# A direct second layer for the fourth token tile of a retention block with a two-layer network, and its groups prepared further ahead

## The chip, the cores and the metric

The kernel runs on one core of a Trainium2 chip. The core has a matrix engine (PE; its weight loads are listed apart as PEld), a vector engine (DVE), an activation engine (ACT), a general engine (POOL), and a queue engine (SP) that issues most of the DMA transfers. Each engine works through its own list of instructions in order; semaphores make one wait for another. The metric is the device time of one execution in microseconds (us). Unless said otherwise, times in the text are counted from the first instruction of the profiled execution.

## The reference

Eight batches of 576 tokens, eight heads of 64. For each head: scores q k^T / 8, multiplied by a decay gamma^(i-j) for j <= i and 0 else, times v. The heads side by side give x with 4608 rows and 512 columns, which goes through two layers:

```python
def _attn_ref(q, k, v):
    scores = scale * np.matmul(q, k.transpose(0, 1, 3, 2))
    ret = scores * Dmat[None, :, :, :]        # gamma[h] ** (i - j), lower triangle
    return np.matmul(ret, v)

def _moe_ref(x, w_in, w_out):                 # w_in 512x2048, w_out 2048x512
    h = x @ w_in
    g = h * np.cos(h)
    return g @ w_out
```

Inputs and output are float32; the kernel multiplies in bfloat16 and sums in float32.

## The kernel before

**Groups.** The 4608 tokens are 36 groups of 128. `load` (L117) issues the DMAs of a group's q, k and v on SP, 256 KB each; group 22 and three others lie across two batches and are loaded in halves. `prep` scales q and k by powers of gamma (L140) and casts v to bfloat16 (L156), on POOL, in the later groups with the cast on ACT. `transposes` (L167) brings the scaled q and k into the layout of the score matmuls; from group 6 on this is one DMA transpose per group, issued on SP, which waits for POOL's two scalings. Five buffers hold raw q, k, v; eight hold prepared groups.

**Attention.** `scores` (L195, then the masked copy on DVE, L207), `state` and `states` (L231, L266: the running sum of k^T v, added up on DVE, L285 and L287) and `attn_out` (L333 `own`, L319 `carried`, then a copy to `xT` on ACT, L350). `scores2(g)` makes the scores of two groups in the banks a and b. `unit7(g, ...)` makes the states of g+1 and g+2, the output of groups g and g+1, and, where `more` is true, the scores of g+2 and g+3.

**Token tiles.** Ten tiles, of 512, 256, 256 and seven times 512 rows; they are numbered from 0, so tile 3 has rows 1024 to 1535 and its groups are 8 to 11. For each tile comes the first layer, `mm1` (eight blocks: PE L365, cosine on ACT L373, product to `gT` on DVE L374), and then the second. Tiles 0 to 2 have a direct second layer (`mm2`, L382): for each of the row blocks of 128, sixteen matmuls of 512 columns are summed in one bank, copied by ACT and stored, and `feed(s)` follows. Attention for the next tile is put between these matmuls by a list `todo` of positions. Tiles from `S7` = 3 on make the product g @ w_out from seven products of half size (`mm2_seven`, L517: 112 matmuls of 256 columns). These need sums of quarters of w_out (`w_sums`, DVE L418, two of them written over w_out itself) and of gT (`g_sum`, L445, on POOL, some on DVE). `sums_after(n, i)` says behind which block of the first layer these are issued; in the tiles after the first two of the seven-product kind the second halves follow in `late_sums`, at the second product. The products come in the order 3, 4, 5, 2, 1, 7, 6, and a dictionary `at` says ahead of which of them attention is put.

**What sets the order.** Nothing is rescheduled: every engine keeps the order in which the program was written (`manual_schedule`). So SP's queue has loads, transposes and stores in the order in which `feed` and the stores issue them, and POOL has preparations and sums in the order of the calls. `feed(s)`, called at each store of row block s, prepares groups up to a number that depends on s, issues their transposes, and then loads further groups. On SP each transfer also waits until the one eight places ahead has landed. PSUM has tags a, b, m (two banks each) and n, st (one each); a block of the first layer holds its tag until DVE's product is done.

Of the kernel before, what the change touches and what calls it, by code (L numbers as in the profile page):

```python
# [17 lines left out]
def kernel(  # L18
# [16 lines left out]
    nc = tc.nc  # L35
    P = 128
# [17 lines left out]
    assert sum(widths) == NTOK  # L54
    starts = [sum(widths[:n]) for n in range(len(widths))]
    N_PE_T = 6
    S7 = 3
    LD = 5

    consts = ctx.enter_context(tc.tile_pool(name="consts", bufs=1))  # L60
# [70 lines left out]
    def prep(g, early=False, kv_first=False):  # L131

        c = g % PER
        fk, fv = (tiles.pop(("f" + n, g)) for n in "kv")
        qks = nat.tile([P, 2, H, D], BF16, tag="qks", name="qks")
        vb = nat.tile([P, H, D], BF16, tag="vb", name="vb")
        qkT = trp.tile([P, 2 * HG, P], BF16, tag="qkT", name="qkT")

        def scaled(eng, m, f, by):
            eng.tensor_tensor(  # L140
                out=qks[:, m].rearrange("p (b a) d -> p a b d", a=2),
                in0=f.rearrange("p (a b) d -> p a b d", a=2),
                in1=by[:, c, :].rearrange("p (a b) -> p a b", a=2).unsqueeze(3).to_broadcast(
                    [P, 2, HG, D]
                ),
                op=ALU.mult,
            )

        if not early and not kv_first:
            scaled(nc.gpsimd, 0, tiles.pop(("fq", g)), gq)  # L150
        scaled(nc.vector if g == 3 else nc.gpsimd, 1, fk, gk)
        if early:
            tiles["fv", g] = fv
        else:
            copy_v = nc.scalar.copy if g > starts[S7] // P + 17 else nc.gpsimd.tensor_copy
            copy_v(vb, fv)  # L156
            if c == MIX and g > PER:
                copy_v(v_odd[HP:, g // PER % 2], fv[HP:])
        if kv_first:
            scaled(nc.gpsimd, 0, tiles.pop(("fq", g)), gq)  # L160
        qT = qT4[:, :, g * P : (g + 1) * P] if early else qkT[:, :HG, :]
        tiles["a", g] = (qks, vb, qkT, qT)
# [213 lines left out]
    def mm2(n, tsi, et):  # L376
        gT = tiles["g", n]
        if et == 0:
            bank = {0: "nmnm", 1: "nm", 2: "mn"}[n][tsi]
            tiles["o", tsi] = psum.tile([P, DM], F32, tag=bank, name="o")  # L380
        ps = tiles["o", tsi]
        nc.tensor.matmul(  # L382
            ps,
            lhsT=gT[:, et, tsi * P : (tsi + 1) * P],
            rhs=w_out_sb[:, et, :],
            start=(et == 0),
            stop=(et == ET - 1),
        )
        if et == ET - 1:
            s = starts[n] // P + tsi  # L390
            ot = op.tile([P, DM], F32, tag="oabcd"[1 + s % 4], name="ot")
            nc.scalar.copy(ot, ps)  # L392
            nc.sync.dma_start(out[s * P : (s + 1) * P, :], ot)
            feed(s)
# [30 lines left out]
    def g_sum(n, x, e0, e1):  # L425

        gT = tiles["g", n]
        a, b, op_ = {
            5: ((0, 0), (0, 1), ALU.add),
            2: ((1, 0), (1, 1), ALU.add),  # L430
            1: ((0, 0), (1, 1), ALU.add),
            7: ((0, 1), (1, 1), ALU.subtract),
            6: ((1, 0), (0, 0), ALU.subtract),
        }[x]
        if ("gs", n, x) not in tiles:
            tiles["gs", n, x] = sump.tile([P, E2, 256], BF16, tag=f"gs{x}", name=f"gs{x}")
        on_dve = x == 5 or (n, x) == (S7, 2) or (n, x, e0) in (
            (S7, 1, 4), (last, 1, 0), (last, 2, 4)
        )
        step = e1 - e0 if on_dve else 2  # L440
        for e in range(e0, e1, step):
            i0, i1 = (
                gT[:, k * E2 + e : k * E2 + e + step, r * 256 : (r + 1) * 256] for r, k in (a, b)
            )
            i = (nc.vector if on_dve else nc.gpsimd).tensor_tensor(  # L445
                out=tiles["gs", n, x][:, e : e + step], in0=i0, in1=i1, op=op_
            )
            if on_dve:
                tiles["gate"] = i
            elif "gate" in tiles:  # L450
                tc.add_manual_dep(
                    i.ins,
                    tiles.pop("gate").ins.name,
                    mybir.DependencyInfo(mybir.DependencyClass.Sync, mybir.DependencyReason.DATA),
                    reason="port free",
                )

    def sums_after(n, i):

        if n == S7:  # L460
            if i < 4:
                w_sums(3 + i % 2, i // 2 * 4, i // 2 * 4 + 4)
            elif i < 6:
                g_sum(n, 5, i % 4 * 4, i % 4 * 4 + 4)
                if i == 5:
                    g_sum(n, 6, 0, 4)
            elif i == 7:
                g_sum(n, 2, 0, E2)
                g_sum(n, 1, 4, E2)
                g_sum(n, 1, 0, 4)  # L470
                for e in (0, 4):
                    g_sum(n, 7, e, e + 4)
                prep_next(kv_first=True)
                g_sum(n, 6, 4, E2)
        elif n == S7 + 1 and i in (3, 7):
            for x in (5, 2, 1):
                g_sum(n, x, i - 3, i + 1)
            for x in (7, 6) if i == 7 else ():
                for e in (0, 4):
                    g_sum(n, x, e, e + 4)  # L480
        elif i == 3:
            for x in (5, 2, 1, 7, 6) if n < last else (5, 1, 2, 7, 6):
                g_sum(n, x, 0, 4)
        elif i == 7 and n == last:
            late_sums(n)
# [113 lines left out]
    def feed(s):  # L599

        nonlocal loaded, prepared, transposed
        before = loaded
        n, r = divmod(s - starts[S7] // P, 4)
        if n >= 0:
            while prepared < min(NG, starts[S7] // P + 10 + 4 * n + ((0, 1, 2, 4) if n else (-1, 0, 1, 4))[r]):
                prep_next()
            while transposed < prepared:
                transposes(transposed)
                transposed += 1
            ahead = starts[S7] // P + 14 if n == 0 and r < 3 else prepared + LD  # L610
            while loaded < min(NG, prepared + LD, ahead):
                load(loaded)
                loaded += 1
            return
        while True:
            while prepared < min(loaded, 2 * s + 7, s + 11, starts[S7] // P + 8):
                prep(prepared)
                prepared += 1
                if transposed < N_PE_T:
                    transposed += 1  # L620

            if N_PE_T <= transposed < min(prepared, s + 11) and (
                transposed <= loaded - 2 or loaded == NG or (s > 3 and loaded == before)
            ):
                transposes(transposed)
                transposed += 1
            elif loaded < min(NG, 2 * s + 8, s + 13):
                load(loaded)
                loaded += 1
            else:  # L630
                break
# [148 lines left out]
    for n, w in enumerate(widths):  # L780

        if n in (0, 3):
            halves = [(h, et) for et in range(0, ET, 4) for h in range(2)]
            if n == 3:
                halves.sort()
            blocks = [(et, half * 256, 256) for half, et in halves]
        elif n == 1:
            blocks = [(et, half * P, P) for half in range(2) for et in (0, 8)]
        else:
            m = 1024 // w  # L790
            blocks = [(et, 0, w) for et in range(0, ET, m)]
            if n > S7:
                blocks = [(e + k * E2, 0, w) for e in range(0, E2, m) for k in range(2)]
        banks = {0: "abmabmab", 1: "bmba", 2: "bmab", 3: "mamabmab"}.get(n, "abmabmab")
        for i, (et, c0, cw) in enumerate(blocks):
# [25 lines left out]
        elif n == 1:  # L821
            todo = pair(6, "ab", 16, 27)
        elif n == 2:
            todo = [(11, lambda: scores2(g)), (25, lambda: unit(g, "m", soon=True))]
            late += [lambda: unit(g + 2, "b", False)]
        else:
            at = {}
            if n + 1 < len(widths):
                at = {
                    4: lambda then, off: unit7(g, "st", True, lambda: late_sums(n), off),  # L830
                    1: lambda then, off: unit7(g + 2, "n", True, then),
                }
                if n in (3, 4):
                    at = {
                        5: lambda then, off: (then(), scores2(g)),
                        1: lambda then, off: unit7(g, "n", True, then),
                        6: lambda then, off: unit7(g + 2, "b", n > 3, then),
                    }
            mm2_seven(n, at)
            continue  # L840
        todo.sort(key=lambda u: u[0])
# [42 lines left out]
```

## Time and profile before

| | us |
|---|---|
| three runs | 299.29, 300.03, 300.26 |
| median | 300.03 |
| profiled execution, first to last instruction (its own time is given as this span) | 298.2 |
| busy in it: PE / DVE / ACT / POOL | 287.1 / 207.9 / 135.9 / 209.4 |
| first layer of tile 3 | 84.20 to 99.55 |
| second layer of tile 3 | 99.55 to 116.78 |
| tile 4 | 116.78 to 149.83 |
| tile 5 | 149.83 to 179.84 |
| tile 6 | 180.00 to 209.35 |

Busy time of PE counts modelled ends of matmuls that overlap, so the spacing of a dense row of matmuls (its time divided by their number) says what one costs, not the mean duration. In the timeline a line is start, duration, engine, line, operation, output <- inputs, shapes, count, and in brackets the idle time ahead with what ended it. SPq rows are issues; when a transfer lands is told apart from that, as "DMA to landing".

### The profile page before, as it was taken

What the parts mean: (1) busy time and instruction counts of PE and PEld (TensorE: products, weight loads), DVE (VectorE), ACT (ScalarE), POOL (GpSimd) and SP (SyncE); (2) the same over time, 40 slices, a digit from 0 to 9 for tenths busy, and PEclk for the clock granted to TensorE, in tenths of its full rate; (3) what the DMA queues carried; (4) which work ended last, traced back from release to release, by engine and by line L of the source; (5) the groups of instructions that cost most, each with busy time, mean ns of one, the idle gap of its engine ahead of it and who ended that gap; (6) DMA issues with size and microseconds to landing.
All of it is one profiled execution on the core that took longest, in us unless ns stands there. A gap on an engine that the chain in (4) does not pass through costs nothing.

```text
span 298.2 us, 7384 instructions
## 1 busy us (share of the span) xinstructions
PE 287.1 (96%) x3113; PEld 195.3 (65%) x3113; DVE 207.9 (70%) x245; ACT 135.9 (46%) x167; POOL 209.4 (70%) x214
## 2 busy tenths in 40 slices
PE   8899999999999999979999999999999999999995
PEld 3478646848578786448744875488448845874584
DVE  5677637564579994788848874887489757935872
ACT  2656433514255432642346554546464446425620
POOL 2750066436445599997999999599959946980693
PEclk9999999999999999999999999999999999999999
DMA  7999999999999999999999997998690260031013
GB/s 203 212 209 206 209 214 213 200 243 208 208 174 222 211 239 213 217 279 176 198 224 229 209 200 183 212 208 201 122 194 2 73 143 0 2 106 36 0 44 99
DMA packets 154304, 50.28 MB, mean 169 GB/s; under 512 B 140832, under 2 KB 153248, under 8 KB 154272
## 3 DMA queue, kind: packets, MB, share of 16 engines
q1 hardware_dynamic: 149504, 45.10, 77.2%
q0 software_dynamic: 4224, 4.19, 8.5%
q8 instruction: 24, 0.39, 0.6%
q10 hardware_dynamic: 544, 0.52, 0.5%
q14 instruction: 8, 0.07, 0.1%
HBM read 36.70 MB, written 9.44 MB: 155 GB/s over the span
## 4 chain that ended last, share of the span: by engine, by line
PE 43%; POOL 25%; SPq 13%; DMA 8%; DVE 5%; issue 3%; ACT 1%; POOLq 0%; DVEq 0%
PE h L365 22%; POOL gs L445 17%; PE o L517 11%; SPq L117 8%; POOL qks L140 6%; PE o L382 5%; SPq L167 4%; DVE gT L374 3%; DMA fk<-in_k_dram 2%; DMA w_in_sb<-in_moe_w_in_dram 2%; DMA qkT<-qks 2%; POOL vb L156 2%; DVE gs L445 2%; DMA fv<-in_v_dram 1%; ACT cosh L373 1%
## 5 line engine op out<-in xcount | busy, mean ns | idle before, releaser
L445 POOL TENSOR_TENSOR gs<-gT 128x512 bf16<-128x512 bf16 x102 | 116.3, 1180 | 29.4 <-DVE gs L445 29.4
L365 PE MATMUL h<-xT,w_in_sb 128*128 128x512 bf16 (+2 forms) x832 | 127.6, 313 | 2.6 <-DVE gT L374 1.8
L374 DVE TENSOR_TENSOR gT<-h,cosh 128x1024 bf16<-128x1024 f32 x72 | 87.8, 1223 | 43.7 <-ACT cosh L373 40.7
L373 ACT ACTIVATE cosh<-h,half_pi 128x1024 f32<-128x1024 f32 x72 | 80.2, 1114 | 72.2 <-PE h L365 69.8
L365 PEld LDWEIGHTS <-w_in_sb 128*128 128x128 bf16 x832 | 75.9, 98 | 51.6 <-issue 3.0
L140 POOL TENSOR_TENSOR qks<-fq,gq 128x512 bf16<-128x512 f32 x32 | 34.0, 1062 | 40.9 <-DMA fq<-in_q_dram 40.9
L517 PEld LDWEIGHTS <-gs 128*128 128x128 bf16 x576 | 53.6, 98 | 10.1 <-POOL gs L445 2.9
L140 POOL TENSOR_TENSOR qks<-fk,gk 128x512 bf16<-128x512 f32 x35 | 37.3, 1066 | 8.0 <-DMA fk<-in_k_dram 7.4
L207 DVE TENSOR_TENSOR ret<-sc,tri 128x1024 bf16<-128x1024 f32 x32 | 38.1, 1217 | 2.8 <-PE sc L195 2.7
L517 PE MATMUL o<-ws,gs 128*128 128x256 bf16 (+1 forms) x352 | 39.1, 268 | 0.7 <-POOL gs L445 0.5
L382 PE MATMUL o<-w_out_sb,gT 128*128 128x512 bf16 x128 | 30.1, 380 | 0.0
L517 PE MATMUL o<-w_out_sb,gT 128*128 128x256 bf16 x224 | 26.6, 273 | 0.1
L517 PE MATMUL o<-w_out_sb,gs 128*128 128x256 bf16 x224 | 26.1, 273 | 0.5 <-POOL gs L445 0.4
L537 DVE TENSOR_TENSOR ot<-o,ot 128x512 f32<-128x512 f32 (+2 forms) x25 | 14.9, 603 | 14.7 <-PE o L517 14.5
L517 PEld LDWEIGHTS <-gT 128*128 128x128 bf16 x224 | 21.4, 98 | 4.7 <-DVE gT L374 0.7
L350 ACT CAST xT<-ov 128x1024 bf16<-128x1024 f32 (+1 forms) x18 | 16.5, 917 | 16.1 <-PE ov L319 13.9
L445 DVE TENSOR_TENSOR gs<-gT 128x1024 bf16<-128x1024 bf16 (+1 forms) x18 | 20.4, 1148 | 0.3
L382 PEld LDWEIGHTS <-gT 128*128 128x128 bf16 x128 | 11.8, 98 | 12.5
L156 POOL CAST vb<-fv 128x512 bf16<-128x512 f32 x22 | 14.3, 651 | 4.4 <-DMA fv<-in_v_dram 4.2
L564 ACT COPY ot<-o 128x512 f32<-128x512 f32 x7 | 4.1, 586 | 20.5 <-PE o L517 20.5
L392 ACT COPY ot<-o 128x512 f32<-128x512 f32 x8 | 4.7, 588 | 17.4 <-PE o L382 17.4
L537 DVE TENSOR_TENSOR ot<-ot,o 128x512 f32<-128x512 f32 x14 | 9.6, 684 | 4.0 <-ACT ot L569 2.4
(70 smaller groups left out, 175.8 us busy)
## 6 DMA issues: line engine op xcount, KB each, us to landing
out_dram<-ot SPq DMA_DIRECT2D x35, 256.0 KB, 4.0
fk<-in_k_dram SPq DMA_DIRECT2D x32, 256.0 KB, 5.2
fv<-in_v_dram SPq DMA_DIRECT2D x32, 256.0 KB, 5.2
fq<-in_q_dram SPq DMA_DIRECT2D x30, 256.0 KB, 4.5
w_in_sb<-in_moe_w_in_dram POOLq DMA_DIRECT2D x4, 512.0 KB, 8.9
w_out_sb<-in_moe_w_out_dram POOLq DMA_DIRECT2D x4, 512.0 KB, 16.2
fq<-in_q_dram SPq DMA_DIRECT2D x8, 128.0 KB, 4.0
fk<-in_k_dram SPq DMA_DIRECT2D x8, 128.0 KB, 4.4
```

The lines of the kernel that those rows point to most:

```text
L117: i = nc.sync.dma_start(f[p0:p1], src[b, :, s0 : s0 + p1 - p0, :].rearrange("h s d -> s h d"))
L140: eng.tensor_tensor(out=qks[:, m].rearrange("p (b a) d -> p a b d", a=2), in0=f.rearrange("p (a b) d -> p a b d", a=2), in1=by[:, c, :].re ...
L156: copy_v(vb, fv)
L207: nc.vector.tensor_tensor(out=ret.rearrange("p a b i -> p (a b) i"), in0=ps.rearrange("p a b i -> p (a b) i"), in1=mask.unsqueeze(1).to_br ...
L350: evac(tiles["x", n][:, :, t0 : t0 + len(gs) * P], ps.rearrange("p c x i -> p c (x i)"))
L365: nc.tensor.matmul(ps[:, j, :], lhsT=w_in_sb[:, dg, (et + j) * P : (et + j + 1) * P], rhs=xT[:, dg, c0 : c0 + w], start=(dg == 0), stop=(d ...
L373: nc.scalar.activation(cosh, ps, ACTF.Sin, bias=half_pi, scale=1.0)
L374: nc.vector.tensor_mul(gT[:, et : et + m, c0 : c0 + w], ps, cosh)
L382: nc.tensor.matmul(ps, lhsT=gT[:, et, tsi * P : (tsi + 1) * P], rhs=w_out_sb[:, et, :], start=(et == 0), stop=(et == ET - 1),)
L445: i = (nc.vector if on_dve else nc.gpsimd).tensor_tensor(out=tiles["gs", n, x][:, e : e + step], in0=i0, in1=i1, op=op_)
L517: nc.tensor.matmul(dst[i], lhsT=lhs[:, e, j * P : (j + 1) * P], rhs=rhs[:, e, c0:c1], start=(x in (3, 4, 1, 7) and e == 0 and (i == 0 or l ...
L537: pend.append(lambda: nc.vector.tensor_tensor(out=out_, in0=in0, in1=in1, op=op_))
```

## The change

Tile 3 goes from the seven products to the direct second layer: `S7` is 4. In its `todo` stand the scores of groups 12 and 13 ahead of matmul 4, the unit of groups 12 and 13 ahead of matmul 24, and that of groups 14 and 15 ahead of matmul 46; the latter now also makes the scores of groups 16 and 17, which stood in tile 4. Tile 4 is the first with seven products: the sums of w_out that stood in tile 3's first layer stand in its first layer, and its attention and its sums take the form of the later tiles. `feed` prepares up to group 19, 21, 23, 23 at the four row blocks of tile 3 (16, 17, 18, 21 before, with one of them prepared among the sums), and loads five further. `feed` counts its tiles from `starts[3]` as before; the limits of the tiles after that are unchanged.

```diff
-    S7 = 3
+    S7 = 4
@@ prep
-            copy_v = nc.scalar.copy if g > starts[S7] // P + 17 else nc.gpsimd.tensor_copy
+            copy_v = nc.scalar.copy if g > 25 else nc.gpsimd.tensor_copy
@@ mm2
-            bank = {0: "nmnm", 1: "nm", 2: "mn"}[n][tsi]
+            bank = {0: "nmnm", 1: "nm", 2: "mn", 3: ("n", "st", "n", "st")}[n][tsi]
@@ g_sum
-        on_dve = x == 5 or (n, x) == (S7, 2) or (n, x, e0) in (
-            (S7, 1, 4), (last, 1, 0), (last, 2, 4)
-        )
+        on_dve = x == 5 or (n, x, e0) in ((last, 1, 0), (last, 2, 4))
@@ sums_after
-        if n == S7:
-            if i < 4:
-                w_sums(3 + i % 2, i // 2 * 4, i // 2 * 4 + 4)
-            elif i < 6:
-                g_sum(n, 5, i % 4 * 4, i % 4 * 4 + 4)
-                if i == 5:
-                    g_sum(n, 6, 0, 4)
-            elif i == 7:
-                g_sum(n, 2, 0, E2)
-                g_sum(n, 1, 4, E2)
-                g_sum(n, 1, 0, 4)
-                for e in (0, 4):
-                    g_sum(n, 7, e, e + 4)
-                prep_next(kv_first=True)
-                g_sum(n, 6, 4, E2)
-        elif n == S7 + 1 and i in (3, 7):
-            for x in (5, 2, 1):
-                g_sum(n, x, i - 3, i + 1)
-            for x in (7, 6) if i == 7 else ():
-                for e in (0, 4):
-                    g_sum(n, x, e, e + 4)
-        elif i == 3:
+        if n == S7 and i < 4:
+            w_sums(3 + i % 2, i // 2 * 4, i // 2 * 4 + 4)
+        if i == 3:
             for x in (5, 2, 1, 7, 6) if n < last else (5, 1, 2, 7, 6):
                 g_sum(n, x, 0, 4)
@@ feed
-        n, r = divmod(s - starts[S7] // P, 4)
+        n, r = divmod(s - starts[3] // P, 4)
-            while prepared < min(NG, starts[S7] // P + 10 + 4 * n + ((0, 1, 2, 4) if n else (-1, 0, 1, 4))[r]):
+            while prepared < min(NG, starts[3] // P + 10 + 4 * n + ((0, 1, 2, 4) if n else (2, 4, 6, 6))[r]):
                 prep_next()
...
-            ahead = starts[S7] // P + 14 if n == 0 and r < 3 else prepared + LD
-            while loaded < min(NG, prepared + LD, ahead):
+            while loaded < min(NG, prepared + LD):
                 load(loaded)
@@ the loop over tiles
-            if n > S7:
+            if n >= S7:
                 blocks = [(e + k * E2, 0, w) for e in range(0, E2, m) for k in range(2)]
...
+        elif n == 3:
+            todo = [
+                (4, lambda: scores2(g)), (24, lambda: unit7(g, "b")), (46, lambda: unit7(g + 2, "b"))
+            ]
...
-                if n in (3, 4):
-                    at = {
-                        5: lambda then, off: (then(), scores2(g)),
-                        1: lambda then, off: unit7(g, "n", True, then),
-                        6: lambda then, off: unit7(g + 2, "b", n > 3, then),
-                    }
```

## The prediction

> **What bounds the kernel now.** I read the page first, then the busy times by stage, then each engine's timeline around tile 3 (rows 1024 to 1535). The page:
>
> ```profile
> span 298.2 us, 7384 instructions
> ...
> PE 287.1 (96%) x3113; PEld 195.3 (65%) x3113; DVE 207.9 (70%) x245; ACT 135.9 (46%) x167; POOL 209.4 (70%) x214
> ...
> DMA  7999999999999999999999997998690260031013
> ...
> ```
>
> PE is busy 96%, so a change pays where it removes PE work or a PE wait, and costs where it adds one. The DMA row says that until two thirds of the span the 16 engines have no spare time: what is asked for earlier there does not come earlier. The stages: first layer of tile 3, its second layer, the same two of tile 4, then tiles 5 and 6 whole (columns: window, length, busy PE, PEld, DVE, ACT, POOL, clock, DMA share, GB/s).
>
> ```profile
> 84.20:99.55 15.35, 15.35 (x178) 13.49 (x177) 13.40 (x17) 9.29 (x9) 8.76 (x9) 1.00 1.33 183
> 99.55:116.78 17.23, 16.57 (x274) 13.42 (x272) 14.31 (x19) 6.12 (x10) 15.35 (x15) 1.00 1.20 244
> 116.78:132.53 15.75, 13.97 (x66) 6.26 (x64) 11.72 (x9) 7.80 (x7) 15.12 (x18) 1.00 1.26 243
> 132.53:149.83 17.30, 16.58 (x289) 13.73 (x288) 13.95 (x17) 5.82 (x9) 15.58 (x15) 1.00 0.97 188
> 149.83:179.84 30.01, 29.61 (x339) 19.79 (x336) 21.78 (x24) 16.09 (x21) 29.87 (x30) 1.00 1.08 219
> 180.00:209.35 29.35, 29.35 (x322) 19.59 (x320) 20.99 (x23) 16.37 (x21) 26.27 (x25) 1.00 0.91 192
> ```
>
> A tile without waits takes 29.35 us (tile 6, PE full). Tile 4 takes 33.05, tile 5 30.01. So at most 3.7 + 0.7 = 4.4 us can be won there. Where tile 4 loses is in PE's and DVE's timelines: PE waits 1.78 for one gT, because a DVE sum of 0.69 elsewhere takes 3.33 while POOL prepares groups without a break.
>
> ```profile
> 126.30 3.33 DVE L445 TENSOR_TENSOR gs<-gT 128x1024 bf16<-128x1024 bf16 x1
> ```
> ```profile
> 130.81 1.89 PE L365 MATMUL h<-xT,w_in_sb 128*128 128x512 bf16 x8 [1.78 <-DVE gT L374]
> ```
>
> SP's queue, in which every load, transpose and store is issued in order:
>
> ```profile
> 115.06 0.88 SPq L544 DMA_DIRECT2D out_dram<-ot  x1
> 116.06 2.02 SPq L167 DMA_TRANSPOSE qkT<-qks  x1
> 118.13 0.58 SPq L117 DMA_DIRECT2D fq<-in_q_dram  x1
> ...
> 129.42 4.05 SPq L167 DMA_TRANSPOSE qkT<-qks  x3
> ```
>
> The 116.06 row is group 16's transpose, behind the store of row block 8 (115.06) and the loads up to group 19. POOL, which prepares groups and makes the sums, in tiles 4 and 5:
>
> ```profile
> 135.91 13.42 POOL L445 TENSOR_TENSOR gs<-gT 128x512 bf16<-128x512 bf16 x12 [1.72 <-DVE gs L445]
> ...
> 160.79 18.34 POOL L445 TENSOR_TENSOR gs<-gT 128x512 bf16<-128x512 bf16 x16
> ```
>
> 16 sums take 18.34 us; begun 10.96 us into tile 5 they end just ahead of PE's last product.
>
> **The change, part by part.** The numbers are for this execution, span 298.2. The runs' median 300.03 (299.29 to 300.26) is 1.8 more, which I take as what lies around the span, and add at the end. The two programs' order on SP is the same up to the last load of group 19, so SP's rows up to 115.06 hold for the changed kernel.
>
> First layer of tile 3. Four weight sums (0.68, 0.68, 0.68, 0.94) and two gs sums (1.52, 0.68) leave DVE. PE is busy 15.35 of 15.35 there, so this gains 0. PE ends it at 99.55 as before.
>
> Second layer on PE. 112 matmuls of 256 columns (48 in 5.35 us: 0.1115 each, 12.49) become 64 of 512 columns (45 in 9.71: 0.2158 each, 13.81): +1.3. Scores of groups 16 and 17 move from tile 4 into tile 3: 0.45 more here, 0.45 less there.
>
> The first scores stand after 4 matmuls now. Group 12's begin at 99.55 + 4 x 0.216 = 100.4; group 13's need bank b, which DVE frees when the last gT is done: last cosh at 99.79 + 1.12, gT 1.23, 102.2. A PE wait of 1.5 us. From below 0 (DVE far ahead, which its 1.23 after the cosh excludes), from above 2; 1.5 taken. It is swallowed by the next one.
>
> The transposes. After group 13's scores (102.4) come 20 matmuls (4.3), the unit of groups 12 and 13 (states 0.37, own 0.45, carried 0.30, scores 0.45: 1.6), 22 matmuls (4.75) and 1.1 of the next unit: PE wants group 16's scores at 114.2. They need the transpose of group 16, which by the order on SP is the issue right behind the store of block 8: the slot at 116.06 with its 4.7 us to landing (answer for that issue), so 120.8. Group 17's transpose takes the slot at 118.13. For its landing the nearest rows are the three in a row at 129.42, with 3.3 to 5.1: 121.4 to 123.2. I take 122.0, nearer to the short end because these two of three landed after 3.3 and 3.4. PE stands from 114.2 to 122.0, save 0.2 of work. What is queued behind it on PE: 0.2 of scores, 18 matmuls (3.9) and all of tile 4. Tile 4 starts at 126.1 instead of 116.78: **+9.3**.
>
> No wait of 6 us on PE is in this trace, and the granted clock is 1.00 in all six windows. What the matmuls cost after one lies between the same 0.216 and, by the slowest row of this trace (14 idle matmuls of the start in 5.32 us, 0.38 each), 18 x 0.16 = 3 us more. I take nothing, as PE is not what ends tile 4 (below), and keep 3 for the range.
>
> The Trainium skill, "TensorE: Matmul & The Clock Gate", Part 1, says that after an idle window of about 3.4 us the array runs at half clock until it was busy for as long; this speaks against the change. By it, an estimate: 3.4 us at half rate, 1.7 us lost, tile 4 from 127.8 on. No row here shows such a drop inside the kernel.
>
> Tile 4's sums. On POOL they now stand behind the preparation of groups 20 to 23 (before: behind 21), whose loads stand on SP behind four transposes. These are issued at 116.06, 118.13, then 1.38 apart as in the 129.42 row: SP is free at 122.2. The first load lands 4.2 later (answers for loads: 3.9 to 5.1), 126.4. Of the remaining loads to group 23's v, 8 are whole and 6 are halves (group 22 straddles two batches; 0.65 each in SP's rows). For a whole load the rows give 0.98 (six from 118.13 to 123.98), 1.27 (twelve from 137.88 to 153.13) and 1.5 (three from 140.88 to 145.38). I take 1.27, the longest run: 126.4 + 8 x 1.27 + 6 x 0.65 = 140.5. The cast of v 0.61, 16 sums 18.34, PE's last four matmuls 0.5 (149.33 to 149.83 in tile 4 before): tile 4 ends at **160.0**. With 0.98 it is 157.6, with 1.5 161.8. PE alone would need 126.1 + 29.35 = 155.5, so it waits in the last four products for some 4.5 us together. Before, the tile ended at 149.83: +10.2.
>
> The DVE sums moved into tile 4's first layer (four weight sums, one gs) meet POOL preparing groups. Their price there is between 0.68 each and the 3.33 of the row above; PE lost 1.78 to one such. POOL now stops for each load (three ops of 2.7 us per 3.8 us), so I take under 1 us each, hidden by the 4.5 us. Without that cover all of it counts.
>
> The Trainium skill, "SBUF — State Buffer", section "SBUF: two separate sides", calls the port pair of DVE and POOL an exclusive lock held for a whole instruction. The 3.33 row is longer than one of POOL's (1.03) at the end of which it should pass, so the trace is harsher than the rule; by the rule each moved sum loses at most 1.03.
>
> Tile 5. By then groups 20 to 25 are prepared and loads are ahead; POOL has only two preparations (5.2 us) before its sums and PE finds them in time: 29.35 instead of 30.01, -0.7. Tiles 6 to 9 and the end are as before, 0.
>
> The other edits: the casts still go to ACT from group 26 on, and the direct layer's four evacuations (ACT, 0.59) and stores run beside PE: 0.
>
> Sum: 9.3 (to tile 4) + 0.9 (in tile 4) - 0.7 = +9.5. Span 307.7, time 309.5.
>
> **The rivals.** *Faster:* the two transposes are there by 114.2, and the loads of group 23 by 128. Then tile 3 costs 13.8 + 1.5 + 0.45 + 3.1 + 0.2 = 19.1 (+1.9), tile 4 falls to 29.35 (-3.7), tile 5 -0.7: 297.5. For it speaks that tile 4's waits are real and its POOL load shrinks; against it SP's slot at 116.06, which nothing in the change moves. It decides if SP clears group 19's loads 6.6 us earlier. 4%.
>
> *Only the first wait:* transposes as above, loads at 0.98 or better, sums not late: tile 4 ends at 155.5, +5.7 - 0.7: 305.0. The 118.13 rows speak for it, the full DMA row against. It decides if group 23 is prepared by 136.5. 17%.
>
> *Worse:* loads at 1.5 each, or PE slow after its wait (3) together with DVE sums that hold it up (two of 1.78): tile 4 ends at about 162: +12.2 - 0.7, 311.5, and more if both. 20%.
>
> That nothing changes is left with 1%; the likeliest, as summed, has 58%, its own range 307.5 to 311.
>
> **How the numbers follow.** 309.5 is the likeliest case. The range reaches to 304.5, just under the second rival, and to 314, the third with both its parts; it leaves out the faster rival and some of each tail, about 15 in 100. A difference under 0.3% (0.9 us) can't be told from none here. Faster 0.04, same 0.01, slower 0.95.
>
> **What would show it.** PE's timeline should have a gap of 6 us and one of about 1 ended by the landing of qkT, some 15 us into tile 3's second layer, and one of 1.5 near its start ended by DVE gT. POOL's 16 sums of tile 4 should begin at about 141, directly after a v cast, and PE should have waits on gs in products 2, 1, 7, 6 there. Tile 5 should take 29.4. I am wrong if the slot behind the store of block 8 comes before 110, or if PE's longest wait is on something other than qkT.

## The result and the profile after

The changed kernel takes 312.88 us (median of four runs, 311.87 to 313.29) against 300.14 for the kernel before beside it: the ratio is 1.0423, interval 1.0395 to 1.045. The profiled execution has a span of 311.4 and a time of 313.14, so 1.7 us lie around the span. The forecast was slower, 309.5, with a range of 304.5 to 314.

The page of the changed kernel, the lines that answer to those shown of before, and the clock row:

```profile
span 311.4 us, 7246 instructions
...
PE 290.8 (93%) x3040; PEld 193.2 (62%) x3065; DVE 199.6 (64%) x235; ACT 136.4 (44%) x168; POOL 198.1 (64%) x204
...
PEclk9999999999999995999779999999999999999999
DMA  8999999999999999999999921799492232022003
...
```

The PE share falls from 96% to 93% because PE waits; the clock row, all 9 before, now has a 5 and two 7s. Busy times by stage of the changed kernel: first layer of tile 3, its second layer, the same two of tile 4, then tiles 5 and 6 (window, length, busy PE, PEld, DVE, ACT, POOL, granted clock, DMA share, GB/s):

```profile
84.90:100.41 15.51, 15.51 (x177) 13.59 (x177) 9.52 (x12) 9.29 (x9) 8.37 (x10) 1.00 1.28 201
100.41:127.54 27.13, 19.69 (x253) 10.06 (x255) 10.68 (x12) 6.12 (x10) 10.85 (x13) 0.87 1.08 219
127.54:142.18 14.64, 13.93 (x65) 6.26 (x65) 11.39 (x12) 8.39 (x8) 11.66 (x13) 1.00 1.23 206
142.18:163.62 21.44, 18.48 (x257) 14.87 (x256) 12.29 (x15) 5.81 (x9) 21.44 (x21) 0.84 1.29 210
163.62:193.06 29.44, 29.34 (x337) 19.84 (x337) 21.95 (x24) 15.99 (x21) 21.21 (x20) 1.00 0.76 153
193.06:222.41 29.35, 29.25 (x321) 19.62 (x321) 21.00 (x23) 16.37 (x21) 26.23 (x25) 1.00 0.92 181
```

| | before | after | difference |
|---|---|---|---|
| tile 3 begins | 84.20 | 84.90 | +0.7 |
| first layer of tile 3 | 15.35 | 15.51 | +0.2 |
| second layer of tile 3 | 17.23 | 27.13 | +9.9 |
| first layer of tile 4 | 15.75 | 14.64 | -1.1 |
| second layer of tile 4 | 17.30 | 21.44 | +4.1 |
| tile 5 | 30.01 | 29.44 | -0.6 |

The sum is 13.2, the difference of the spans, which are those of one profiled execution of each kernel. The first 0.7 is not of the change: it is a wait of PE for a transpose in tile 2, which some profiled executions have (0.55 to 0.9 us, one of them a variant of the kernel before) and others not. All that is lost lies in the two second layers. PE's timeline there:

```profile
102.89 0.42 PE L195 MATMUL sc<-qkT 64*64 64x128 bf16 x16 [1.25 <-DVE gT L374]
...
120.31 0.64 PE L195 MATMUL sc<-qkT 64*64 64x128 bf16 x16 [4.69 <-DMA qkT<-qks]
121.75 0.64 PE L195 MATMUL sc<-qkT 64*64 64x128 bf16 x16 [0.80 <-DMA qkT<-qks]
122.72 4.98 PE L382 MATMUL o<-w_out_sb,gT 128*128 128x512 bf16 x17 [0.33 <-issue]
...
152.93 2.14 PE L496 MATMUL o<-w_out_sb,gs 128*128 128x256 bf16 x8 [2.88 <-POOL gs L443]
...
157.64 6.15 PE L496 MATMUL o<-ws,gs 128*128 128x256 bf16 x48
```

Three waits were named ahead and are here: for DVE's last gT at the first scores (1.25), for the transposes of groups 16 and 17 (4.69 and 0.80), and for POOL's sums in product 2 (2.88). The matmuls behind the second and third wait are slow: 17 direct ones take 4.98 us, where PE had done 19 in 4.49 at 103.24, and 48 of the products take 6.15 instead of 5.35 to 5.42. SP's and POOL's timelines show what the waits were for:

```profile
115.24 0.88 SPq L393 DMA_DIRECT2D out_dram<-ot  x1
116.23 5.89 SPq L167 DMA_TRANSPOSE qkT<-qks  x4
122.17 1.50 SPq L117 DMA_DIRECT2D fq<-in_q_dram  x1
```
```profile
127.33 1.04 POOL L140 TENSOR_TENSOR qks<-fq,gq 128x512 bf16<-128x512 f32 x1 [8.13 <-DMA fq<-in_q_dram]
...
138.04 0.67 POOL L156 CAST vb<-fv 128x512 bf16<-128x512 f32 x1 [0.63 <-DMA fv<-in_v_dram]
...
141.81 0.61 POOL L156 CAST vb<-fv 128x512 bf16<-128x512 f32 x1
142.38 18.28 POOL L443 TENSOR_TENSOR gs<-gT 128x512 bf16<-128x512 bf16 x16
```

The four transposes stand behind the store of row block 8 and take SP until 122.1; the first two land 4.0 and 4.1 us after their issue. POOL is idle 8.13 us for the load of group 20, then prepares 20 to 22 as they land; its last wait for a load is that for group 22's v at 138.04. Group 23's preparation follows with no further wait, and only then come the sums of tile 4, with no break.

### The profile page after: what moved, and what is told of

It reads as the page before. It is cut to its first block, busy times and chain, and to the rows that moved or that the text cites. A ratio compares the mean times of both kernels' runs of the same rounds, so it can differ in the third digit from the quotient of the medians.

```text
span 311.4 us, 7246 instructions
## 1 busy us (share of the span) xinstructions
PE 290.8 (93%) x3040; PEld 193.2 (62%) x3065; DVE 199.6 (64%) x235; ACT 136.4 (44%) x168; POOL 198.1 (64%) x204
## 4 chain that ended last, share of the span: by engine, by line
PE 64%; POOL 15%; DMA 9%; SPq 5%; issue 3%; DVE 2%; ACT 1%; POOLq 0%; DVEq 0%
PE h L365 33%; PE o L496 15%; POOL gs L443 13%; PE o L382 9%; SPq L117 4%; DMA fk<-in_k_dram 2%; DMA w_in_sb<-in_moe_w_in_dram 2%; PE sc L195 2%; DMA qkT<-qks 2%; PE ov L333 2%; DMA fv<-in_v_dram 2%; POOL qks L140 1%; DMA fq<-in_q_dram 1%; PE ov L319 1%; PE st L266 1%
## 5 line engine op out<-in xcount | busy, mean ns | idle before, releaser
L443 POOL TENSOR_TENSOR gs<-gT 128x512 bf16<-128x512 bf16 x92 | 105.4, 1184 | 33.6 <-DVE gs L443 33.6
L496 PEld LDWEIGHTS <-gs 128*128 128x128 bf16 x496 | 46.9, 99 | 11.5 <-POOL gs L443 4.8
L382 PE MATMUL o<-w_out_sb,gT 128*128 128x512 bf16 x180 | 43.8, 387 | 1.1 <-issue 0.7
L496 PE MATMUL o<-ws,gs 128*128 128x256 bf16 (+1 forms) x304 | 33.6, 271 | 0.3 <-POOL gs L443 0.2
L382 PEld LDWEIGHTS <-gT 128*128 128x128 bf16 x192 | 18.2, 100 | 20.5 <-issue 2.0
L496 PE MATMUL o<-w_out_sb,gs 128*128 128x256 bf16 x192 | 23.4, 279 | 3.1 <-POOL gs L443 2.9
L496 PE MATMUL o<-w_out_sb,gT 128*128 128x256 bf16 x192 | 22.8, 273 | 0.0
L496 PEld LDWEIGHTS <-gT 128*128 128x128 bf16 x192 | 18.4, 98 | 3.8
L195 PE MATMUL sc<-qkT 64*64 64x128 bf16 (+1 forms) x480 | 11.8, 230 | 7.7 <-DMA qkT<-qks 6.4
L195 PEld LDWEIGHTS <-qkT 64*64 64x64 bf16 (+1 forms) x512 | 9.7, 112 | 12.5 <-DMA qkT<-qks 7.0
L443 DVE TENSOR_TENSOR gs<-gT 128x1024 bf16<-128x1024 bf16 x14 | 14.8, 1066 | 0.2
```

What stands on the lines that cost most here:

```text
L195: nc.tensor.matmul(ps[i0:i1, he, hg, :], lhsT=qkT[d0 : d0 + D, HG + hg, i0:i1], rhs=qT[d0 : d0 + D, hg, :], start=True, stop=True,)
L382: nc.tensor.matmul(ps, lhsT=gT[:, et, tsi * P : (tsi + 1) * P], rhs=w_out_sb[:, et, :], start=(et == 0), stop=(et == ET - 1),)
L443: i = (nc.vector if on_dve else nc.gpsimd).tensor_tensor(out=tiles["gs", n, x][:, e : e + step], in0=i0, in1=i1, op=op_)
L496: nc.tensor.matmul(dst[i], lhsT=lhs[:, e, j * P : (j + 1) * P], rhs=rhs[:, e, c0:c1], start=(x in (3, 4, 1, 7) and e == 0 and (i == 0 or l ...
```

## The experiments

Theory A was that of the prediction: PE's wait for the transposes in tile 3 and POOL's late sums in tile 4 are two limits side by side, so that easing one leaves the other. Rivals: B, that the transposes are the whole loss and the sums only follow; C, that the direct layer's own work costs it. All kernels start from the changed one, but for the last. The ratio is to runs of the kernel before taken beside each (medians 300.14 for the changed kernel, 300.41 for a1 to a4, 299.69 for a5, a6 and b1). The last column is of the profiled execution; in the kernel before it is 116.8, 149.8.

| kernel | time, median and runs | ratio to before, interval | tile 4 begins, ends |
|---|---|---|---|
| changed | 312.88 (311.87 to 313.29) | 1.0423 (1.0395 to 1.045) | 127.5, 163.6 |
| a1, scores back in tile 4 | 313.62 (312.13 to 316.4) | 1.0465 (1.038 to 1.0551) | 119.1, 165.2 |
| a2, groups to 21 only | 308.25 (307.85 to 308.69) | 1.0284 (1.0242 to 1.0326) | 128.1, 158.4 |
| a3, both of these | 305.57 (304.52 to 306.03) | 1.0189 (1.0144 to 1.0235) | 119.1, 155.0 |
| a4, PE kept busy | 311.01 (310.02 to 312.91) | 1.0383 (1.0328 to 1.0439) | 128.4, 161.8 |
| a5, transposes first | 313.31 (312.37 to 313.78) | 1.0449 (1.0421 to 1.0476) | 121.8, 162.8 |
| a6, transposes first and groups to 21 | 304.57 (304.17 to 305.89) | 1.0169 (1.014 to 1.0197) | 123.7, 154.8 |
| a7, small stores | 309.05, one run | | 125.2, 159.5 |
| b1, before with one sum later | 298.82 (298.59 to 299.29) | 0.9971 (0.9958 to 0.9985) | 116.8, 148.9 |

**a1: the scores of groups 16 and 17 back in tile 4.**

```diff
-                (46, lambda: unit7(g + 2, "b"))
+                (46, lambda: unit7(g + 2, "b", False))
...
+                if n == 4:
+                    at = {
+                        5: lambda then, off: (then(), scores2(g)),
+                        1: lambda then, off: unit7(g, "n", True, then),
+                        6: lambda then, off: unit7(g + 2, "b", True, then),
+                    }
...
-        elif i == 7 and n == last:
+        elif i == 7 and n in (4, last):
```

> The changed kernel with the scores of groups 16 and 17, and tile 4's attention, put back into tile 4 (ahead of products 5, 1 and 6). PE then waits for no transpose in tile 3 and tile 4 starts at about 119 instead of 127.5. Theory A (two limits side by side: PE's wait for the transposes, and POOL's sums of tile 4 behind groups 20 to 23, whose loads land by 141): POOL's sums still begin at 142.4 and end at 160.7, so tile 4 ends at 162 to 166 and the time stays at 311 to 315. Rival B (the wait for the transposes is the whole loss, the sums only follow it): the sums come 8 us earlier and the time is about 304. Rival C (the direct layer's matmuls and the moved sums cost it): no change, but also no change of tile 4's start.

The last line of the edit calls the second halves of tile 4's sums behind its first layer, since that tile's attention no longer calls them. Tile 4 begins 8.4 us earlier, at 119.14, and the time does not fall. PE's and POOL's timelines of this kernel show where the gain went:

```profile
143.30 0.61 PE L496 MATMUL o<-w_out_sb,gs 128*128 128x256 bf16 x4 [3.28 <-POOL gs L443]
144.41 0.61 PE L496 MATMUL o<-w_out_sb,gs 128*128 128x256 bf16 x4 [0.50 <-POOL gs L443]
152.15 2.14 PE L496 MATMUL o<-w_out_sb,gs 128*128 128x256 bf16 x8 [7.14 <-POOL gs L443]
```
```profile
142.09 17.78 POOL L443 TENSOR_TENSOR gs<-gT 128x512 bf16<-128x512 bf16 x16
```

The sums begin at 142.09 as before the edit, and PE waits 10.9 us for them in product 2. Rivals B (304) and C (no earlier start) are both out as accounts of the whole loss. A part of C is left: tile 4 still begins 2.4 us later than in the kernel before (116.78).

**a2: groups prepared only up to 21 in tile 3.**

```diff
-... else (2, 4, 6, 6))[r]):
+... else (2, 4, 4, 4))[r]):
```

> The changed kernel, but tile 3 prepares groups only up to 21; 22 and 23 follow tile 4's sums on POOL. Theory A: the wait of about 5.5 us for the transposes stays and tile 4 starts at 127.5, but POOL's sums begin at 138 to 139.5 (as soon as DVE's gs is there), tile 4 ends at 157 to 158 without PE's wait on gs and without the second stretch of half clock: 5.5 us less, 307. Rival B: the sums are not what ends tile 4, 312.9 as before.

4.6 us less. The wait for the transposes stays (5.21 and 0.35), the sums begin 2.9 us earlier, and now DVE's gs releases them, for which the program makes POOL's sums wait, not a preparation:

```profile
139.44 18.30 POOL L443 TENSOR_TENSOR gs<-gT 128x512 bf16<-128x512 bf16 x16 [5.41 <-DVE gs L443]
```

Tile 4 takes 30.34 with a granted clock of 1.00. Of the profiled 5.2 us (163.6 to 158.4) the earlier sums explain 2.9. The other 2.3 lie behind POOL's last sum: tile 4 ends 0.7 us after it here, and 3.0 us after it in the changed kernel. They go with the second stretch of half clock, which is gone together with the long wait on gs; a4 tests this by itself.

**a3: both edits.**

> Both edits together: scores of 16 and 17 back in tile 4, and groups prepared only up to 21 in tile 3. Theory A: tile 4 starts at 119, POOL's sums begin when group 21 is prepared (134) and end at 152.5, tile 4 ends at 154 to 155: 8.5 to 9 us less than the changed kernel, 303.5 to 304.5, more than either edit alone; that leaves some 4 us over the kernel before, of the sums alone. Rival B: the same 304 as with the scores back alone. Rival C: 312.

305.57, 7.3 under the changed kernel, when a1 alone gave nothing and a2 alone 4.6: the transposes' wait is worth 2.7 once the sums are out of the way and nothing while they are not. That is what two limits side by side look like. The sums begin at 132.89, the moment group 21 is prepared, and PE still waits 3.39 for them. The median is 1 us over what was expected; the profiled execution, 304.52, is at the upper end of it. What is left over the kernel before (tile 4 ends 5.2 us later) is not of the sums alone, as was expected: 2.3 us of it are tile 4's later start, 2.9 its length.

**a4: PE kept busy where it waits.** Matmuls of zeros stand ahead of the scores of group 16 and inside product 2 of tile 4.

```diff
-                (46, lambda: unit7(g + 2, "b"))
+                (46, lambda: unit7(g + 2, "b", idle=22))
...
         for e, i in order:
+            if n == S7 and x == 2 and i == 0 and e in (4, 6):
+                warm(psum.tile([P, 2, 512], F32, tag="m", name="idle")[:, 0], {4: 12, 6: 4}[e])
```

> The changed kernel with matmuls of zeros where PE waits: 22 ahead of the scores of group 16 in tile 3 (4.75 us), 12 and 4 inside product 2 of tile 4 (2.6 and 0.9 us). Nothing else moves. If the half clock is a cost of its own (two stretches of 6.8 us in the changed kernel's clock record), the granted clock is 1.00 throughout, the waits end at the same times, tile 4 starts about 1 us earlier and ends with POOL's sums at 161.2 instead of 163.6: 310.4. If the waits alone cost the time, it stays at 312.9; if the added matmuls delay PE, it rises by up to 1.

1.9 us less by the medians, the work between waits unchanged. The runs of the two kernels overlap (310.02 to 312.91 against 311.87 to 313.29), so the time alone does not show the gain; the traces show where it arises. The same window of tile 4 in the changed kernel and then in this one (columns as above; the clock stands after POOL's count):

```profile
152.30:159.20 6.90, 6.19 (x88) 4.29 (x89) 3.31 (x5) 2.21 (x4) 6.90 (x7) 0.51 1.32 208
```
```profile
152.30:159.20 6.90, 6.60 (x112) 4.89 (x111) 3.63 (x6) 2.21 (x4) 6.90 (x7) 1.00 1.02 203
```

Tile 4 now ends at 161.80, 0.9 us behind POOL's last sum (160.94), where it was 3.0 us in the changed kernel. So there it was PE at half clock, behind the sums, that ended tile 4. In tile 3 the cover was not complete: PE still waited 1.15 and 0.59 for the two transposes, and the clock fell for one stretch of 3.4 us at 123.4, when PE was at work again. The expectation of 1.00 throughout was wrong there, and so was that of an earlier start: tile 4 begins 0.8 us later than in the changed kernel.

**a5: preparations and transposes of 16 and 17 ahead of the loads of 18 and 19.**

```diff
-            while prepared < min(loaded, 2 * s + 7, s + 11, starts[3] // P + 8):
+            while prepared < min(loaded, 2 * s + 7, s + 11, starts[3] // P + 10):
```

> The changed kernel, with groups 16 and 17 prepared and their transposes issued on SP one row block of 128 earlier each, ahead of the loads of groups 18 and 19. Theory A: the transposes land at about 112 and 116.5, PE waits for them 1 us at most, tile 4 starts at 119 to 120.5; but POOL's sums still stand behind group 23, whose loads have not moved (141), so tile 4 ends at 162 to 165 as without the edit: 311 to 314. Theory B (the transposes' place is what costs the time): about 304.

The wait shrinks to one of 2.46 us for group 17's transpose, which landed 1 us later than expected, at 117.5; a wait of 1 us at most and a start of tile 4 by 120.5 were expected, and it starts at 121.8. That is still 5.8 us earlier, and the time is 313.31, as with a1. The sums begin at 142.70. So the first wait was eased in two ways, by moving the reader and by moving what it waits for, with the same outcome.

**a6: the same with groups only up to 21.**

> The transposes of 16 and 17 earlier, and groups prepared only up to 21 in tile 3; the scores stay in tile 3 as the change puts them. Theory A: both limits are eased, tile 4 starts at 119.5, POOL's sums begin at 133 and end at 151.5, tile 4 ends at 152.5 to 154: 302 to 304, the least of the kernels with a direct tile 3, still 2 to 4 over the kernel before, since the sums of tile 4 wait for loads that the full DMA engines bring only by 132. If it comes out under 300, that last point is wrong.

304.57, just over the expected 302 to 304. It is the lowest median of the kernels with a direct tile 3, but its runs overlap those of a3, so which of the two is faster is not shown. The sums begin at 135.78, not 133, and the bracket of POOL's row says what held them last, DVE's gs:

```profile
135.78 18.33 POOL L443 TENSOR_TENSOR gs<-gT 128x512 bf16<-128x512 bf16 x16 [1.23 <-DVE gs L443]
```

Group 21 was prepared 1.2 us ahead of that, at 134.6. So here it is not mainly the loads that keep it above the kernel before, as was expected; it is tile 3: tile 4 begins at 123.7, 6.9 us later than before, and takes 31.09, 2.0 less than before.

**a7: small stores.**

```diff
-            nc.sync.dma_start(out[s * P : (s + 1) * P, :], ot)
+            cols = DM // 4 if s < 8 else DM
+            nc.sync.dma_start(out[s * P : (s + 1) * P, :cols], ot[:, :cols])
```

> The changed kernel, storing only the first 128 of 512 columns of the rows 0 to 1023 (the rest of these rows is left unwritten); as many issues on SP, eight times 192 KB less for the DMA engines. If the DMA engines' full load sets the slot of group 16's transpose (theory A), it comes some 0.4 us earlier per store ahead of it: landing at 116.5 to 118.5 instead of 120.3. If SP's issues or POOL's preparations set the slot, it stays at 120.

This kernel leaves three quarters of each of these rows unwritten, so it is of use only to see the queue move. SP's timeline:

```profile
112.85 0.87 SPq L394 DMA_DIRECT2D out_dram<-ot  x1
113.82 4.50 SPq L167 DMA_TRANSPOSE qkT<-qks  x3
```

The transposes are issued from 113.82 instead of 116.23, group 16's lands at 118.3 instead of 120.3, inside what was expected, and group 23's preparation, and with it the sums, come 3.0 us earlier (139.42). With the same issues and fewer bytes the queue moves up, so the load of the DMA engines has a part in setting these slots. Tile 3's second layer began 1.1 us earlier in this execution (99.3 for 100.4), without the wait in tile 2; that this does not move the slot by itself is seen in the kernel before, where the layer began at 99.55 and the slot was at 116.06. The time, 309.05, is that of one run, 3.8 less; the earlier slot is read from one trace.

**b1: the kernel before, with DVE's gs of tile 4 behind the first layer.** The wait of 1.78 us that the prediction had found in the kernel before was not touched by the change's idea, so it was tried by itself.

```diff
-            for x in (5, 2, 1):
-                g_sum(n, x, i - 3, i + 1)
+            for x in (2, 1) if i == 3 else (5,):
+                g_sum(n, x, 0, i + 1)
+            for x in (2, 1) if i == 7 else ():
+                g_sum(n, x, 4, E2)
```

> The kernel before, with the DVE sum of tile 4 (gs5) issued as one piece behind the first layer's last block instead of two halves behind blocks 3 and 7. In the kernel before its first half took 3.33 us beside POOL's unbroken preparations, and PE waited 1.78 for a gT behind it. If that wait was the sum's place, it goes: tile 4 takes 31.5 to 32 instead of 33.05, 298.7 to 299.2. If POOL's sums of tile 4 end the tile anyway, no change: 300.2.

298.82 against 299.69, ratio 0.9971 (0.9958 to 0.9985): 0.3% faster than the kernel before, and the fastest of all. Tile 4 takes 32.07 instead of 33.05, where 31.5 to 32 was expected. The whole sum, twice the elements, now takes 1.67 us on DVE beside a POOL that was busy for the first 0.6 of it and then idle, where half of it took 3.33 beside a busy one:

```profile
133.26 1.67 DVE L445 TENSOR_TENSOR gs<-gT 128x2048 bf16<-128x2048 bf16 x1
```

The wait of 1.78 is gone from PE's first layer; 0.50 of it comes back as a wait on POOL's sums, which are next (a second such wait, 0.28, was there before with 0.27).

## Why the prediction was right, and where its sizes were off

**The first layer of tile 3, the direct layer's work.** As forecast: nothing gained in the first layer; the direct matmuls at 0.22 each where the clock is full.

**The first scores' wait.** 1.25 for 1.5. That the next wait swallows it was not tried by itself.

**The transposes.** PE was ready for group 16's scores at 115.6 (forecast 114.2; 0.9 of the difference is the later start of this execution's second layer). They landed at 120.3 and 121.7 for 120.8 and 122.0. Because SP's order is the same up to that slot, the times of the profile of before could be read off for the changed kernel, to half a microsecond. The premise that under full DMA engines nothing asked for earlier comes earlier is too broad: in a5 the transpose of group 17, put ahead of the loads of group 19, landed 4.2 us earlier (117.5 for 121.7), and POOL began on those loads 3.7 us later (120.3 for 116.6). The second layer of tile 3 took 9.9 more; forecast was 9.3. That these are so close is in part luck. The layer began 0.9 late in this execution, which the wait swallowed, and behind the second landing PE took 5.8 us to the end of the layer for the 4.1 of the forecast, since the clock was at half until 125.0.

**Tile 4's sums.** They began at 142.4 for 141.1, behind group 23 as told; a1 and a5 show that an earlier start of tile 4 on PE, by 8.4 and 5.8 us, hardly moves its end (165.2 and 162.8 for 163.6), a2 that taking groups 22 and 23 from in front of the sums does. The price of the loads held: from the first landing to that of group 23's v it was 14.0 us for the 14.1 summed. Of the 1.3 us, 0.8 is the first load, which landed 5.0 us after its issue, at 127.2, for 4.2 and 126.4. The other 0.5 is POOL: group 23's v landed at 141.2, but POOL took it up at 141.81, as it was still scaling group 23's q and k, behind group 22's v and a second cast of that (L158, 0.96 us), for which the sum had no term.

**Tile 5 and the rest.** 29.44 and 29.35 for 29.35 each.

**What was mis-sized.** The term for PE's speed after a wait: "I take nothing, as PE is not what ends tile 4". For the first wait that was nearly right, since the sums covered what it cost. For the second wait it was wrong: the prediction saw that PE would wait in the last four products for some 4.5 us together and did not ask the same question there. PE waited 2.88 us, all of it in product 2; the waits named for products 1, 7 and 6 did not come, as PE at half clock ran behind the sums. The half clock lasted 6.8 us (152.3 to 159.2), and PE, slowed, ended tile 4 three microseconds after POOL's last sum at 160.7, for the 0.5 that the sum had there. Of the 3.6 us by which tile 4 ended later than forecast (163.6 for 160.0), 1.3 are the sums' later start; most of the other 2.3 is the half clock, since in a4, at full clock, PE ended 0.9 us after the last sum, 2.1 us less. The prediction had kept 3 us for a slow PE in its range, and the measured time lies within it.

The Trainium skill's rule, "TensorE: Matmul & The Clock Gate", Part 1, had been cited for the first wait with 3.4 us at half rate. The trace shows 6.8 us there (118.2 to 125.0), and again 6.8 at the second wait, twice 3.41. The rule's condition, an idle window of about 3.4 us, is stricter than what the runs show: see the last section.

**DVE's moved sums beside POOL.** They took 0.68 to 1.09 each, PE lost 0.66 for a gT; about 1 us at most, as taken. POOL's rows there have pauses of 0.2 to 0.9 us for loads; that these are the reason was not tried by itself.

**The rivals.** The faster one fails at its first condition, the slot on SP; and a5 and a6, which issue these two transposes earlier, show that this was not enough to reach it: a5 gained nothing, and in a6 tile 3 still ended 6.9 us later than before. The "only the first wait" case did not arise in the changed kernel. It is near a2 in form, at 308.25 for the 305.0 that was given; in a2 tile 4 begins 2.0 us later than that rival had it, with half clock behind the first wait and a second layer of tile 3 that began 0.9 late, and takes 1.0 us longer.

## What to carry to other kernels

Work that is moved earlier needs its inputs earlier, so read in the issuing queue where those inputs stand; where the order ahead of that slot stays and the DMA engines are full, the wait can be dated from the old trace, as here to half a microsecond. Look for the second limit as well: here each of two edits that removed or shortened the first wait gained nothing until the sums behind the preloaded groups were freed too. And when a wait of a few microseconds on PE is forecast, give the matmuls behind it two prices, at full and at half clock, at every such wait and not only at the longest.

## What the runs showed that was not expected

The half clock came after shorter waits than 3.4 us, and the length of the wait alone does not decide it. In a6 PE waited once, 2.39 us, and the clock was halved behind it. In a5 it waited 2.46 us at the same place, and the clock stayed full. In a4 two waits of 1.15 and 0.59 us with scores between were enough; the single wait of 1.78 us in the kernel before was not.

The clock records of the traces tell these cases apart. Inside the kernels the stretches of half clock last 3.41, 6.83, 10.24 or 13.65 us, all multiples of 3.41, and where a trace has two of them, their starts lie 10 (changed kernel) or 9 (a7) times 3.41 us apart. So each trace can be cut into windows of 3.41 us, of which some begin where a stretch begins. Two such windows in a row of a6, of a5 and of a4 (PE's busy time is the figure behind the comma, the clock the third from the end):

```profile
114.57:117.98 3.41, 1.02 (x54) 0.76 (x52) 1.98 (x3) 1.62 (x3) 2.08 (x3) 1.00 1.25 280
117.98:121.39 3.41, 3.08 (x23) 1.29 (x17) 1.23 (x1) 0.59 (x1) 0.86 (x1) 0.50 1.20 240
```
```profile
113.32:116.73 3.41, 1.72 (x66) 1.21 (x64) 2.07 (x3) 1.62 (x3) 2.70 (x3) 1.00 1.26 261
116.73:120.14 3.41, 2.48 (x26) 1.34 (x28) 1.22 (x1) 0.59 (x1) 0.00 (x0) 1.00 1.25 230
```
```profile
119.97:123.39 3.42, 1.52 (x36) 0.82 (x36) 1.50 (x2) 0.00 (x0) 0.52 (x1) 1.00 1.02 207
123.39:126.80 3.41, 3.41 (x9) 1.22 (x8) 0.86 (x1) 0.58 (x1) 0.02 (x1) 0.50 1.05 212
```

In a6 the wait fell into one window, in which PE was busy 1.02 of 3.41 us. In a5 it fell across the edge of two, and each of them kept PE busy for longer. Over the complete windows inside the kernels of all ten traces, every window at full clock with PE busy for up to 1.52 us was followed by half clock, and none with 1.63 us or more was; 1.63 is the window of the 1.78 us wait in the kernel before (128.48 to 131.89). A stretch ended behind a window with 2.96 us or more, and went on behind one with 2.94 (a1) or less. These borders are read off these runs, no run was made to find them, and PE's busy time is partly modelled. The edges of the windows lie at a different place in each execution, so which of two waits of 2.4 us was followed by half clock was, as far as these runs show, chance.
